# A seven-product feed-forward stage: another order of its twelve periods, and six weight chunks converted later

## The chip, the cores and the metric

The kernel runs on one core of one Trainium2 chip. The core's engines are TensorE (PE, with its weight loads as PEld), VectorE (DVE), ScalarE (ACT), GpSimd (POOL) and SyncE (SP); the last one issues nearly all transfers, on one queue. The metric is the device time of one execution in microseconds (us); lower is better. Before the change three runs took 952.39, 954.0 and 958.7 us, a median of 954.0 us.

## The reference

Attention over 4 batches of 576 tokens (8 heads of 64), then a gated block with a spatial matrix, then the block that the change is about. Cut to its end:

```python
def _moe2_ref(x, U, V, w_ch1, w_ch2):
    xt = x.transpose(0, 2, 1)
    h = xt @ U @ V
    u = x + h.transpose(0, 2, 1)
    ch = np.maximum(u @ w_ch1, 0.0) @ w_ch2
    return (u + ch).astype(np.float32)
```

Here x is 2304 tokens by 512 features, w_ch1 is 512 by 2048 and w_ch2 2048 by 512. The weights reach the device as 64-bit floats in raw words, and the kernel itself turns them into float32. Every product is made of three matmuls on a high and a low part of each operand.

## The kernel before, in words

The program has three stages. The **attention stage** (0 to 326 us) is written by hand and is not touched. In the **middle stage** (326 to 576 us) the gated block runs batch by batch: `u_step`, `v_step`, `s_step`, `o_step`, then `y_step`, `z_step`, `h_step` for x @ U @ V. TensorE's order is the order of the code there; the other engines' orders come from a scheduler. Beside it, `first_weights` converts the weights: 32 chunks of 128 rows by 512 numbers (`raw`), each with one ScalarE instruction (line 771) and four VectorE instructions (lines 772 to 775); after every second chunk four adds and subtracts (lines 782 to 785) complete seven combinations of blocks in the tile `cb`, two of them on VectorE and two on GpSimd, and `cb` is stored in DRAM (`combo`). `go` paces this: a chunk for every `EVERY` units of its clock.

The **channel stage** (`channel`, 576 to 954 us) computes the two big matrices by a seven-product scheme: instead of eight products of half-size blocks it makes seven, from combinations of the operands. The tokens are cut into 3 passes of 768, the hidden features into 4 weight groups of 512. A `period` is one pass with one group: 7 products with w_ch1 (tiles `r<i>x`, `r<i>y`, `r<i>z` in PSUM), then 7 with w_ch2 (`a<i>X`, and again y and z). A product is 12 matmuls. Before, period i took pass i // 4 and group i % 4, so every period ends with a change of weights, and two (after periods 3 and 7) with a change of pass as well.

- Change of weights (`split`): the seven combinations of both matrices come from `combo` in DRAM through four staging buffers (`YH`, `YL`, two each); ScalarE copies the high part (`w1h`, `w2h`, `setA`), VectorE or GpSimd subtracts to get the low part (`w1l`, `w2l`). For group 0, which returns at each change of pass, the low parts are not computed again: they were stored once (`lows`) and are loaded.
- Change of pass: VectorE makes four combinations of the next tokens (`tu`), ScalarE copies seven high parts and VectorE subtracts seven low parts into `setA`, `XH`, `XL`.

All work of the channel stage is put into one list by `at(t, fn)`, t in units of one product (14 per period), sorted by t; equal t keeps the order of entry. Each engine then works in that order, so an instruction that waits holds all that stand behind it on its engine. For example:

```python
            for t, fn in (
                (1.0, lambda: keep_sum("p1", "x")), (2.0, lambda: add_sum(1, "y", "p1")), (2.5, lambda: relu(1)),
                (3.0, lambda: keep_sum("u2", "x")), (3.4, lambda: high(1, T[1])), (3.9, lambda: low(pool, 1, T[1])),
                (4.0, lambda: keep_sum("p5", "z")), (5.0, lambda: add_sum(3, "x", "p5")),
```

`keep_sum` is a ScalarE copy out of PSUM. The copy of p5 must be done before the sixth product of the period (slot 5, from 5.0 units on) may add to z; the copy of u2 before the fifth (slot 4) may add to x.

The channel stage's first weights come through the tile `tmp` (14 loads, one per combination) as soon as the middle stage's tiles are free; behind their low parts on VectorE stand the four `X<-q` adds of the last but one batch, for which TensorE's transposes `t` wait.

Of the kernel before, what the change touches and what calls it, by code (L numbers as in the profile page):

```python
# [8 lines left out]
F32 = mybir.dt.float32  # L9
# [56 lines left out]
def tile_kernel(ctx: ExitStack, tc: tile.TileContext, qk, vv, tabs, w_in, g_ln, wsgT, b_sg, w_out, u_r, v_r, w1, w2, out):  # L66
# [8 lines left out]
    def bits(ap):  # L75

        return ap.bitcast(U32)
# [672 lines left out]
    LOWS = [dram.tile([P, 7, FG], F32, name=f"lows{c}", bufs=1) for c in range(2)]  # L750
    COMBO = [[dram.tile([P, 7, 2, HF], F32, name=f"combo{c}_{g}", bufs=1) for g in range(NG)] for c in range(2)]

    def first_weights():

        places = [{n: j for j, n in enumerate(at)} for at in (AT1, AT2)]
        jobs = []
        for g in range(NG):
            for c, src in enumerate((w1[:, g * 2 * FG:(g + 1) * 2 * FG], w2[g * FG:(g + 1) * FG])):
                for r in range(2):
                    jobs += [(g, c, r, k, src[k * P:(k + 1) * P]) for k in (r, r + 2)]  # L760
# [6 lines left out]
        def convert(j, t):  # L767

            raw = raws.pop(j).rearrange("p (a b) w -> p a b w", a=2)
            lo, hi, tu = raw[:, :, :, 0], raw[:, :, :, 1], bits(t)  # L770
            nc.scalar.activation(t, hi.bitcast(F32), AF.Abs)  # L771
            nc.vector.tensor_scalar(t, t, F64_LEAST, F64_MOST, ALU.max, ALU.min)
            nc.vector.tensor_scalar(tu, tu, 5, 2, ALU.logical_shift_left, ALU.logical_shift_right)
            nc.vector.scalar_tensor_tensor(tu, hi, 0xC0000000, tu, ALU.bitwise_and, ALU.bitwise_or)
            return nc.vector.scalar_tensor_tensor(tu, lo, 29, tu, ALU.logical_shift_right, ALU.bitwise_or)

        def combine(c, cb):
            at = places[c]
            e, o = nc.vector, nc.gpsimd
            op = {n: cb[:, at[n]] for n in range(1, 8)}  # L780
            a21, s1, s2, s4 = op[7], *((op[5], op[6], op[3]) if c == 0 else (op[5], op[6], op[3]))
            x = e.tensor_tensor(s1, a21, op[4], ALU.add)
            o.tensor_tensor(a21, a21, op[1], ALU.subtract)
            x = e.tensor_tensor(s2, s1, op[1], ALU.subtract)
            o.tensor_tensor(s4, op[2], s2, ALU.subtract)
            return x

        load(0)
        yield
        box = {}  # L790
        for j, (g, c, r, k, _) in enumerate(jobs):
            if j + 1 < len(jobs):
                load(j + 1)
            with ExitStack() as es:
                for x in LAST_D:
                    if x is not None:
                        es.enter_context(tc.issue_after(x.ins))
                at = places[c]
# [3 lines left out]
                m, n = ((1, 7), (2, 4))[k >= 2]  # L802
                LAST_D[0] = convert(j, cb[:, at[m]:at[n] + 1:at[n] - at[m]])
# [23 lines left out]
    def first_u():  # L827

        b11, b12, b21, b22 = (blk(i, j, 0) for i in range(2) for j in range(2))
        T = {}  # L830

        def combo(n, a, b):
            t = raw_tile()[:, :, :TB]
            sub(nc.vector, t, a, b)
            return t
        both = ((1, lambda: b11), (2, lambda: b21), (5, lambda: combo(5, b12, b11)), (6, lambda: combo(6, b22, T[5])),
                (4, lambda: combo(4, b21, T[6])), (7, lambda: combo(7, b12, b22)), (3, lambda: b22))
        for n, fn in both:
            x = T[n] = fn()
            copy(UOP[n][0], x)  # L840
            u_low(nc.gpsimd if n in (1, 2, 3) else nc.vector, n, x)

    def channel(before):

# [10 lines left out]
        def wop(c, n, x, r, a):  # L855
            j = (AT1, AT2)[c].index(n)
            o = r * HF + a * P
            return wslot(c, x, j)[:, o:o + P]

        def tmp():  # L860
            return p3.tile([P, 2, TB], F32, tag="tmp", name="tmp", bufs=6)

        def wide(t):
            return t[:, :, :TB]
# [17 lines left out]
        def split(c, g, j0, j1, t, stage, load, lo, e=None):  # L882
# [16 lines left out]
            at(t, high)  # L899
            if e is None:  # L900
                for a, b in parts:
                    at(lo, lambda a=a, b=b: nc.sync.dma_start(f(wslot(c, 1, a, b - a)), flat(LOWS[c][:, a:b])))
                return
            if e is nc.gpsimd:
                parts_low = [(j, j + 1) for j in range(j0, j1)]
# [3 lines left out]
                at(lo, lambda a=a, b=b: low(a, b))  # L909

        def stage_small():
            return p3.tile([P, 2, TB], F32, tag="tmp", name="tmp", bufs=6).rearrange("p a b -> p (a b)")

        turn = [0]

# [4 lines left out]

        def period(i):

            p, g = divmod(i, NG)
            o = 14 * i
            ps, T = {}, {}
            dve, act, pool = nc.vector, nc.scalar, nc.gpsimd
# [11 lines left out]
                copy(T[n], wide(ps[x]))  # L938

            def add_sum(n, x, m):  # L940
                T[n] = tmp()
                dve.tensor_tensor(T[n], wide(ps[x]), T[m], ALU.add)

            def relu(n):
# [24 lines left out]
            for t, fn in (  # L969
# [16 lines left out]
            if g == NG - 1:  # L986
                for t, a, b in ((12.5, 0, 1), (12.95, 1, 1), (13.4, 0, 0), (14.01, 1, 0)):
                    at(o + t, lambda a=a, b=b: leave(a, b))
            if i + 1 < NPASS * NG:
                h = (g + 1) % NG  # L990
                loads = (2.3, 4.0, 4.5, 6.5, 6.6) if i == 0 else (1.4, 1.8, 3.2, 3.5, 5.0)
                highs = (3.85, 5.45, 6.5, 9.0, 9.4) if i == 0 else (3.85, 4.75, 6.0, 7.0, 9.4)
                for c, j0, j1, load, t, lo, e in (
                    (0, 0, 2, loads[0], highs[0], 4.35, dve), (0, 2, 4, loads[1], highs[1], 10.3, pool),
                    (0, 4, 6, loads[2], highs[2], 11.6, pool), (0, 6, 7, loads[3], highs[3], 12.9, pool),
                    (1, 0, 2, loads[4], highs[4], 14.5, dve), (1, 2, 4, 11.65, 13.0, 15.08, dve),
                    (1, 4, 6, 13.0, 14.4, 16.5, dve), (1, 6, 7, 13.6, 15.4, 17.1, dve),
                ):
                    if h == 0:
                        split(c, h, j0, j1, o + t, stage, o + load, o + 7 * c + j1 + 0.05)  # L1000
                    else:
                        split(c, h, j0, j1, o + t, stage, o + load, o + lo, e)
            if g == NG - 1 and p + 1 < NPASS:
                b11, b12, b21, b22 = (blk(x, y, p + 1) for x in range(2) for y in range(2))
                U = {}

                def combo(n, a, b):
                    U[n] = pr.tile([P, 2, TB], F32, tag="tu", name="tu", bufs=2)
                    sub(dve, U[n], a() if callable(a) else a, b() if callable(b) else b)
                uh = lambda n, x: copy(UOP[n][0], x)  # L1010
                for t, fn in (
                    (1.7, lambda: uh(1, b11)), (2.1, lambda: uh(2, b21)), (2.5, lambda: u_low(dve, 1, b11)),
                    (2.95, lambda: u_low(dve, 2, b21)), (3.4, lambda: combo(5, b12, b11)), (3.85, lambda: combo(6, b22, U[5])),
                    (4.45, lambda: uh(6, U[6])), (5.25, lambda: uh(5, U[5])), (9.9, lambda: uh(3, b22)),
                    (14.5, lambda: u_low(dve, 6, U[6])), (14.95, lambda: u_low(dve, 5, U[5])),
                    (15.4, lambda: sub(dve, U[5], b12, b22)), (15.85, lambda: sub(dve, U[6], b21, U[6])),
                    (15.9, lambda: uh(7, U[5])), (16.45, lambda: u_low(dve, 7, U[5])), (16.8, lambda: uh(4, U[6])),
                    (16.9, lambda: u_low(dve, 3, b22)), (17.35, lambda: u_low(dve, 4, U[6])),
                ):
                    at(o + t, fn)  # L1020
            return ps

        for c in range(2):
            for j in range(7):
                t = -20 + 2 * (7 * c + j) / 2
                split(c, 0, j, j + 1, t, stage_small, t - 4, t + 0.5, nc.vector if j % 2 else nc.gpsimd)
                at(t + 4, lambda c=c, j=j: nc.sync.dma_start(LOWS[c][:, j], f(wslot(c, 1, j))))
        for i in range(NPASS * NG):
            ps = period(i)
            if i == 0:  # L1030
                before(at, ps)
# [175 lines left out]
```

## Time and profile before

| what | value |
|---|---|
| runs | 952.39, 954.0, 958.7 us |
| profiled execution | 956.1 us, of it 954.3 us span |
| TensorE busy | 895.8 us, 94% of the span |
| VectorE busy | 773.2 us, 81% |
| ScalarE, GpSimd busy | 492.6 us, 468.1 us |
| mean granted TensorE clock | 0.977 of full speed |

The page gives busy time per engine, and the chain that ended last: from 834 us on it is TensorE's products alone, one after the other. A timeline row reads: start, duration, engine, line, operation, written tile <- read tiles, shape, count, and in brackets the idle time of that engine just before and what ended it. SPq is SyncE's queue; its rows are issues of transfers, not their landing.

### The profile page before, as it was taken

To read this page: it belongs to the slowest core of one execution; us is meant where nothing else is said; L and a number is where in the kernel's file an instruction comes from. 1 tells how busy PE (TensorE), PEld (TensorE's weight loads), DVE (VectorE), ACT (ScalarE), POOL (GpSimd) and SP (SyncE) were. 2 spreads that over 40 slices of the span, in tenths; PEclk is the share of its full clock that TensorE was granted. 3 is DMA by queue.
4 is the path that set the end of the run, shared out by engine and by line. 5 is a ranking of instruction groups with operands and counts; after the bars stand their busy time and mean duration, and the time that the engine had idled before them with its cause. 6 is when DMAs were issued, how large, how long until landed. Compare 5 with 4: busy or idle time off the path is not lost. (4 is left out here: it accounts for less than half of the span.)

```text
span 954.3 us, 14383 instructions
## 1 busy us (share of the span) xinstructions
PE 895.8 (94%) x5279; PEld 811.3 (85%) x5279; DVE 773.2 (81%) x964; ACT 492.6 (52%) x749; POOL 468.1 (49%) x365
## 2 busy tenths in 40 slices
PE   9999999999999897997988759999999999799998
PEld 4677888788777897995988759999889999799997
DVE  6667799888995498997889965898879888887877
ACT  4565666676675634434324344445644565356441
POOL 6996777877644644553446441443114324032440
PEclk9999999999999998997999979999999999999999
DMA  6787876878633304654455284333772346634511
GB/s 194 195 198 179 212 205 158 215 169 188 177 102 110 111 8 151 195 167 144 153 170 175 83 295 150 111 101 113 229 265 79 117 137 218 213 118 136 155 56 67
DMA packets 90386, 148.33 MB, mean 155 GB/s; under 512 B 31606, under 2 KB 49292, under 8 KB 90316
## 3 DMA queue, kind: packets, MB, share of 16 engines
q1 hardware_dynamic: 90016, 147.34, 52.5%
q8 instruction: 42, 0.69, 0.3%
q14 instruction: 28, 0.23, 0.1%
q10 hardware_dynamic: 300, 0.08, 0.0%
HBM read 106.40 MB, written 23.14 MB: 136 GB/s over the span
## 5 line engine op out<-in xcount | busy, mean ns | idle before, releaser
L213 DVE TENSOR_REDUCE MX<-sm 128x1 f32<-128x576 f32 (+1 forms) x160 | 117.0, 747 | 37.4 <-PE sm L208 32.1
L277 PE MATMUL pv<-pc,VV 128*65 128x288 f32 (+1 forms) x516 | 145.7, 405 | 0.0
L250 PE MATMUL st<-Q,K 65*128 65x288 f32 (+3 forms) x640 | 126.5, 320 | 3.2 <-DMA Q<-mt 1.9
L250 PEld LDWEIGHTS st<-Q,K 65*128 65x128 f32 (+3 forms) x640 | 95.0, 178 | 18.0 <-DMA Q<-mt 2.5
L253 ACT ACTIVATE pc<-st 128x576 f32<-128x576 f32 x129 | 83.1, 645 | 31.5 <-PE st L250 29.1
L277 PEld LDWEIGHTS pv<-pc,VV 128*65 128x65 f32 (+1 forms) x516 | 69.2, 136 | 29.1 <-issue 0.2
L822 POOL TENSOR_TENSOR r7l<-tmp,r7h 128x768 fp32r<-128x768 f32 x12 | 25.6, 2130 | 126.5 <-ACT r7h L819 37.4
L822 POOL TENSOR_TENSOR r1l<-tmp,r1h 128x768 fp32r<-128x768 f32 x12 | 23.2, 1930 | 130.1 <-ACT r1h L819 110.0
L208 PE MATMUL sm<-K,Q 128*128 128x288 f32 (+1 forms) x320 | 72.1, 315 | 1.2 <-ACT pc L253 0.6
L172 POOL TENSOR_TENSOR Q<-raw,Q 128x576 fp32r<-128x576 f32 x30 | 45.7, 1523 | 30.1 <-ACT Q L167 30.0
L771 ACT ACTIVATE cb<-raw 128x512 f32<-128x512 f32 x32 | 21.5, 674 | 71.3 <-DMA raw<-in_w 61.4
L208 PEld LDWEIGHTS sm<-K,Q 128*128 128x128 f32 (+1 forms) x320 | 50.1, 178 | 7.3 <-DVE MX L213 0.9
L153 POOL TENSOR_TENSOR raw<-raw,tab 128x576 f32<-128x576 f32 x31 | 50.6, 1631 | 2.5 <-DMA raw<-in_qk 2.5
L330 DVE TENSOR_TENSOR X<-stage,rb 64x576 f32<-64x576 f32 x30 | 47.5, 1584 | 1.6 <-DMA rb<-rr 1.1
L155 POOL TENSOR_TENSOR raw<-raw 128x576 f32<-128x576 f32 x31 | 47.6, 1537 | 0.5
L587 PE MATMUL u<-XH,setA 128*128 128x288 f32 x256 | 47.6, 303 | 0.0
L154 POOL TENSOR_TENSOR raw<-raw,tab 128x576 f32<-128x576 f32 x31 | 44.4, 1431 | 0.0
L819 ACT ACTIVATE w2h<-YL 128x1024 fp32r<-128x1024 f32 (+1 forms) x22 | 18.6, 844 | 48.1 <-DMA YL<-combo 44.6
L587 PE MATMUL m<-WS,VH 128*128 128x288 f32 x192 | 34.6, 304 | 6.6 <-ACT ug L658 2.8
L587 PE MATMUL v<-setA,XH 128*128 128x512 f32 x128 | 39.6, 391 | 1.3 <-DVE X L689 1.3
L587 PEld LDWEIGHTS u<-XH,setA 128*128 128x128 f32 x256 | 39.8, 196 | 0.3
L819 ACT ACTIVATE w2h<-YH 128x1024 fp32r<-128x1024 f32 x22 | 23.2, 1056 | 31.3 <-DMA YH<-combo 20.1
(1111 smaller groups left out, 2630.2 us busy)
## 6 DMA issues: line engine op xcount, KB each, us to landing
YH<-combo SPq DMA_DIRECT2D x44, 512.0 KB
raw<-in_qk SPq DMA_DIRECT2D x31, 576.0 KB
raw<-in_w SPq DMA_DIRECT2D x32, 512.0 KB
combo<-cb SPq DMA_DIRECT2D x16, 896.0 KB
YL<-combo SPq DMA_DIRECT2D x22, 512.0 KB
K<-Q SPq DMA_DIRECT2D x30, 288.0 KB
YL<-combo SPq DMA_DIRECT2D x22, 256.0 KB
VV<-in_vv SPq DMA_DIRECT2D x16, 320.0 KB
```

Of the source, the lines that this page charges most:

```text
L153: lambda: e.tensor_tensor(raw[:, 0], raw[:, 0], tab[:, 0], ALU.mult),
L154: lambda: e.tensor_tensor(raw[:, 1], raw[:, 1], tab[:, 1], ALU.mult),
L155: lambda: e.tensor_tensor(raw[:, 0], raw[:, 0], raw[:, 1], ALU.add),
L172: nc.gpsimd.tensor_tensor(Q2[:, :S], rot, f(Q1), ALU.subtract)
L208: nc.tensor.matmul(ps[:TS[t], n, :HALF], Q1[:, t * P:t * P + TS[t]], K1[:, n * HALF:(n + 1) * HALF], start=True, stop=True)
L213: nc.vector.tensor_reduce(MXs[h % 2][:TS[t], t:t + 1], ps[:TS[t], :, :HALF], AX.XY, ALU.max)
L250: nc.tensor.matmul(ps[:kk, n, :HALF], l[:, c * P:c * P + kk], r[:, ns], start=st, stop=not st)
L253: nc.scalar.activation(h2(pc[:kk]), ps[:kk, :, :HALF], AF.Exp, scale=0.125)
L277: nc.tensor.matmul(o, l, r, start=(c == 0 and j == 0), stop=(c == NC - 1 and j == len(pr) - 1))
L330: nc.vector.tensor_tensor(X[b][rows, pr], STAGE.pop(h - 1 + a)[:D], RB[i][:, a], ALU.mult)
L587: nc.tensor.matmul(o, l, rr, start=(first and j == 0), stop=(last and j == n - 1))
L822: return e.tensor_tensor(out, a, b, ALU.subtract)
```

## The change

1. **Order of periods.** A table gives pass and group of each period: (0,0), (0,1), (0,2), (1,2), (1,0), (1,1), (2,1), (2,0), (2,2), (2,3), (0,3), (1,3). Four ends of periods change the pass and keep the weights (after 2, 5, 9 and 10); seven change the weights and keep the pass.
2. **Kept operands.** Low parts of groups 0 to 2 are stored (nine of fourteen slots each), and loaded when the group returns; the other five are computed again, on GpSimd. The token combinations of passes 0 and 1 are stored (`u`) and fetched when the pass returns, in periods 9 and 10.
3. **Conversion.** `EVERY` is 6.5 instead of 5.0, and only 26 of the 32 chunks are converted in the middle stage. The last six are converted in the channel stage, as twelve half chunks (`words`) at the times of `LATE`, with one buffer for the words and one for the combinations. All four combining operations run on VectorE.
4. The temporaries `tmp` have 4 buffers instead of 6; T[1] has a buffer of its own.

```diff
-    EVERY = 5.0
+    EVERY, EARLY = 6.5, 26
...
+    ORDER = [(0, 0), (0, 1), (0, 2), (1, 2), (1, 0), (1, 1), (2, 1), (2, 0), (2, 2), (2, 3), (0, 3), (1, 3)]
+    KEPT = [(0, 0), (0, 1)] + [(1, j) for j in range(7)]
...
+    def combine(c, cb):
+        at = PLACES[c]
+        e = nc.vector
+        op = {n: cb[:, at[n]] for n in range(1, 8)}
+        a21, s1, s2, s4 = op[7], op[5], op[6], op[3]
+        e.tensor_tensor(s1, a21, op[4], ALU.add)
+        e.tensor_tensor(a21, a21, op[1], ALU.subtract)
+        e.tensor_tensor(s2, s1, op[1], ALU.subtract)
+        return e.tensor_tensor(s4, op[2], s2, ALU.subtract)
...
+    LATE = (1, 0.1), (3, 0.1), (4, 0.1), (4, 2.1), (4, 4.1), (5, 0.1), (6, 2.0), (6, 3.9), (7, 0.1), (7, 2.1), (7, 4.1), (8, 0.1)
...
-            p, g = divmod(i, NG)
+            p, g = ORDER[i]
+            q, h = ORDER[i + 1] if i + 1 < len(ORDER) else (p, g)
...
+            if i > 0 and g not in [x for _, x in ORDER[:i]] and g < NG - 1:
+                for c, j in KEPT:
+                    at(o + (0.05 if c == 0 else 3.5), lambda c=c, j=j: nc.sync.dma_start(LOWS[c][g][:, j], f(wslot(c, 1, j))))
+            if h != g:
+                fresh = h not in [x for _, x in ORDER[:i]]
...
-                    if h == 0:
+                    if fresh or (c, j0) not in KEPT:
+                        split(c, h, j0, j1, o + t, stage, o + load, o + lo, e)
+                    else:
                         split(c, h, j0, j1, o + t, stage, o + load, o + 7 * c + j1 + 0.05)
...
+                def fetch(n):
+                    U[n] = block()
+                    nc.sync.dma_start(U[n], UKEPT[q][n])
...
+        def fetch(m):
+            raws[m] = pr.tile([P, HF, 2], U32, tag="words", name="words", bufs=1)
+            nc.sync.dma_start(raws[m].rearrange("p n w -> p (n w)"), parts[m][3])
...
+        def done(m):
+            c, r, _, _ = parts[m]
+            combine(c, cbs[m // 4])
+            nc.sync.dma_start(COMBO[c][NG - 1][:, :, r], cbs[m // 4])
+        at(10.0, lambda: fetch(0))
+        for m, t in enumerate(LATE):
+            t = 14 * t[0] + t[1]
+            at(t - 0.1, lambda m=m: begin(m))
+            at(t, lambda m=m: raws[m][1]())
+            if m + 1 < len(parts):
+                at(t + 1.0, lambda m=m: fetch(m + 1))
+            if m % 4 == 3:
+                at(t + 0.75, lambda m=m: done(m))
```

`begin` is the ScalarE instruction of a half chunk, `raws[m][1]` its four VectorE instructions.

How the orders change, at three places. First ScalarE in the middle stage, second batch, about 434 to 444 us of the trace: `ug<-v` are the activations of `v_step`, `cb<-raw` the conversions, `YH<-t` the copies for which the next `z_step` waits. Before:

```order
L771 ACTIVATE cb<-raw 128x512
L578 ACTIVATE ug<-v_2_4557 128x1024
L578 ACTIVATE ug<-v_4_4620 128x512
L771 ACTIVATE cb<-raw 128x2x256
L710 ACTIVATE YH<-t_0_4656 128x1024
L710 ACTIVATE YH<-t_2_4669 128x1024
L771 ACTIVATE cb<-raw 128x2x256
```

Now:

```order
L578 ACTIVATE ug<-v_2_4543 128x1024
L773 ACTIVATE cb<-raw 128x512
L578 ACTIVATE ug<-v_4_4606 128x512
L710 ACTIVATE YH<-t_0_4634 128x1024
L710 ACTIVATE YH<-t_2_4647 128x1024
L639 ACTIVATE ug<-ug,bmv,brs 128x512 x2
```

The conversion that stood right ahead of `YH<-t` stands one activation earlier, and the next one behind.

Second VectorE at the end of the middle stage, about 556 to 574 us of the trace. `X<-w` are the adds after `o_step`, `w1l`, `setA`, `w2l` low parts of the channel stage's first weights, `X<-q` the adds that the transposes wait for. Before:

```order
L689 TENSOR_TENSOR X<-w_1_5633,X 128x576
L822 TENSOR_TENSOR w1l<-tmp,w1h 128x512
L689 TENSOR_TENSOR X<-w_2_5670,X 128x576
L822 TENSOR_TENSOR w1l<-tmp,w1h 128x512
L822 TENSOR_TENSOR setA_71<-tmp,setA_70 128x512
L689 TENSOR_TENSOR X<-w_3_5696,X 128x576
L822 TENSOR_TENSOR w2l<-tmp,w2h 128x512 x3
L738 TENSOR_TENSOR X<-q_0_5817,X 128x576
```

Now:

```order
L689 TENSOR_TENSOR X<-w_2_5635,X 128x576
L829 TENSOR_TENSOR XH<-raw,XH 128x768
L689 TENSOR_TENSOR X<-w_3_5661,X 128x576
L829 TENSOR_TENSOR w1l<-tmp,w1h 128x512 x2
L829 TENSOR_TENSOR setA_71<-tmp,setA_70 128x512
L829 TENSOR_TENSOR w2l<-tmp,w2h 128x512 x3
L738 TENSOR_TENSOR X<-q_0_5777,X 128x576
```

All six low parts now stand behind the last `X<-w`.

Third the start of period 4 as it is now. ScalarE (`tmp<-r4x` the copies of p1 and u2, `tmp<-r4z` that of p5):

```order
L826 ACTIVATE w2h<-YL 128x512
L773 ACTIVATE cb_6111<-words 128x256
L826 ACTIVATE t_6933<-t_6933 128x768
L826 ACTIVATE tmp<-r4x 128x768
L826 ACTIVATE r1h<-t_6933 128x768
L826 ACTIVATE w1h<-YH 128x1024
L773 ACTIVATE cb_6981<-words 128x256
L826 ACTIVATE tmp<-r4z 128x768
```

and SyncE's queue at the same place:

```order
L1071 DMA words<-in_w 128x512
L901 DMA YH<-combo_1_3345 128x1024
L901 DMA YL<-combo_1_3345 128x1024
L914 DMA w1l<-lows_1_3325 128x1024
L1083 DMA combo_3_3347<-cb_6111 896x1x256
L1071 DMA words<-in_w 128x512
```

Two half chunks stand among ScalarE's copies, the second one directly ahead of p5; its fetch stands behind the store of the combination that ends with the half chunk before it.

## Rows read from the trace of the kernel before

**Rows 1.** The page: span, and busy time of each engine with its instructions.

```profile
span 954.3 us, 14383 instructions
PE 895.8 (94%) x5279; PEld 811.3 (85%) x5279; DVE 773.2 (81%) x964; ACT 492.6 (52%) x749; POOL 468.1 (49%) x365
```

**Rows 2.** Windows, middle stage: length, busy by engine, granted clock, DMA share, GB/s.

```profile
326.16:575.62 249.46, 216.69 (x1404) 203.97 (x1404) 213.57 (x302) 99.67 (x152) 120.52 (x103) 0.93 0.46 152
440.00:460.00 20.00, 16.32 (x94) 14.84 (x95) 12.77 (x22) 10.23 (x16) 6.32 (x8) 0.75 0.36 126
```

**Rows 3.** Timeline, 430 to 444 us: fetches of raw chunks and what waited.

```profile
430.63 0.33 SPq L765 DMA_DIRECT2D raw<-in_w  x1
...
433.97 0.69 ACT L771 ACTIVATE cb<-raw 128x512 f32<-128x512 f32 x1 [4.84 <-DMA raw<-in_w]
434.32 0.53 SPq L806 DMA_DIRECT2D combo<-cb  x1
...
434.96 2.54 SPq L765 DMA_DIRECT2D raw<-in_w  x2
...
441.59 0.66 ACT L771 ACTIVATE cb<-raw 128x512 f32<-128x512 f32 x1 [5.53 <-DMA raw<-in_w]
...
443.21 0.80 PE L726 MATMUL z<-YH,U 128*128 128x512 f32 x1 [6.39 <-ACT YH L710]
```

**Rows 4.** Groups of the conversion (busy, mean ns), and lines by min/median/max ns.

```profile
L772 DVE TENSOR_SCALAR cb<-cb 128x512 f32<-128x512 f32 x32 | 22.4, 699 | 6.5 <-ACT cb L771 6.4
L775 DVE SCALAR_TENSOR_TENSOR cb<-raw,cb 128x512 uint32<-128x512 uint32 x32 | 28.4, 889 | 0.7
L783 POOL TENSOR_TENSOR cb<-cb 128x256 f32<-128x256 f32 x16 | 15.2, 951 | 39.5 <-DVE cb L782 23.6 <-issue 15.5 <-POOL XL L431 0.4
L775 DVE SCALAR_TENSOR_TENSOR cb<-raw,cb x32: 674/692/2221, 355.2 to 541.0; 128x512 uint32<-128x512 uint32 x32
L782 DVE TENSOR_TENSOR cb<-cb x16: 393/423/1533, 359.3 to 543.3; 128x256 f32<-128x256 f32 x16
```

**Rows 5.** Timeline, 562 to 575 us: the start of the channel stage.

```profile
563.18 0.74 DVE L689 TENSOR_TENSOR X<-w,X 128x576 f32<-128x576 f32 x1
...
567.04 0.44 SPq L889 DMA_DIRECT2D tmp<-combo  x1
...
571.49 2.75 DVE L738 TENSOR_TENSOR X<-q,X 128x576 f32<-128x576 f32 x4
571.51 0.63 ACT L819 ACTIVATE w2h<-tmp 128x512 fp32r<-128x512 f32 x1 [0.67 <-DMA tmp<-combo]
...
572.29 3.03 PE L708 MATMUL t<-ident,X 128*128 128x128 f32 x13 [7.78 <-DVE X L738]
```

**Rows 6.** Timeline of PE, both changes of pass: first matmuls of halves of periods.

```profile
670.40 0.51 PE L877 MATMUL r3x<-setA,w1h 128*128 128x384 f32 x2
...
709.25 0.98 PE L877 MATMUL r4x<-setA,w1h 128*128 128x384 f32 x2 [2.13 <-ACT tmp L819]
...
721.37 0.52 PE L877 MATMUL a4X<-r1h,w2h 128*128 128x384 f32 x2
...
736.05 0.51 PE L877 MATMUL r5x<-setA,w1h 128*128 128x384 f32 x2
...
794.73 0.51 PE L877 MATMUL r7x<-setA,w1h 128*128 128x384 f32 x2
...
846.47 0.52 PE L877 MATMUL a8X<-r1h,w2h 128*128 128x384 f32 x2
```

**Rows 7.** Timeline, 701 to 708 us: a staged block and the copy that waited.

```profile
701.90 0.44 SPq L889 DMA_DIRECT2D YH<-combo  x1
...
707.45 1.06 ACT L819 ACTIVATE w2h<-YH 128x1024 fp32r<-128x1024 f32 x1 [5.60 <-DMA YH<-combo]
```

**Rows 8.** Groups of the channel stage: one VectorE add, one ScalarE copy.

```profile
L963 DVE TENSOR_TENSOR X<-a3X,X 128x768 f32<-128x768 f32 x4 | 3.8, 956 | 1.2 <-PE a3X L877 1.1
L819 ACT ACTIVATE r3h<-tmp 128x768 fp32r<-128x768 f32 x12 | 10.2, 846 | 15.9 <-DVE tmp L942 15.9
```

More of the change, by code (lines that the diff above doesn't have):

```diff
@@ L765, in load @@
             return nc.sync.dma_start(raws[j].rearrange("p n w -> p (n w)"), jobs[j][-1])
[L767 to L786, printed above, removed]
         load(0)
@@ L790, in first_weights @@
         box = {}
-        for j, (g, c, r, k, _) in enumerate(jobs):
-            if j + 1 < len(jobs):
+        for j, (g, c, r, k, _) in enumerate(jobs[:EARLY]):
+            if j + 1 < EARLY:
                 load(j + 1)
@@ L797, in first_weights @@
                         es.enter_context(tc.issue_after(x.ins))
-                at = places[c]
+                at = PLACES[c]
                 if k < 2:
@@ L801, in first_weights @@
                 cb = box[0]
-                m, n = ((1, 7), (2, 4))[k >= 2]
-                LAST_D[0] = convert(j, cb[:, at[m]:at[n] + 1:at[n] - at[m]])
+                m, n = BLOCKS[k >= 2]
+                begin, rest = words(raws.pop(j).rearrange("p (a b) w -> p a b w", a=2), cb[:, at[m]:at[n] + 1:at[n] - at[m]])
+                begin()
+                LAST_D[0] = rest()
                 if k >= 2:
@@ L858, in wop @@
             return wslot(c, x, j)[:, o:o + P]
+        TMPS = 4
         def tmp():
-            return p3.tile([P, 2, TB], F32, tag="tmp", name="tmp", bufs=6)
+            return p3.tile([P, 2, TB], F32, tag="tmp", name="tmp", bufs=TMPS)
         def wide(t):
@@ L911, in stage_small @@
         def stage_small():
[L912 removed]
+            return tmp().rearrange("p a b -> p (a b)")
         turn = [0]
@@ new lines, in period @@
+            if q == p:
+                return ps
+            U = {}
+            uh = lambda n, x: copy(UOP[n][0], x() if callable(x) else x)
+            block = lambda: stage()[:, :2 * TB].rearrange("p (a b) -> p a b", a=2)
+            if q in [x for x, _ in ORDER[:i]]:
+                def fetch(n):
+                    U[n] = block()
+                    nc.sync.dma_start(U[n], UKEPT[q][n])
+                for n, load, t, lo in (
+                    (1, 0.6, 1.9, 3.5), (2, 1.15, 2.4, 3.95), (6, 2.55, 3.95, 4.4), (5, 3.15, 4.6, 14.1), (7, 4.1, 5.4, 14.55),
+                    (3, 4.5, 6.3, 15.0), (4, 4.95, 7.2, 15.45),
+                ):
+                    at(o + load, lambda n=n: fetch(n))
+                    at(o + t, lambda n=n: uh(n, U[n]))
+                    at(o + lo, lambda n=n: u_low(dve, n, U[n]))
+                return ps
@@ new lines, in period, with combo @@
+            b11, b12, b21, b22 = (blk(x, y, q) for x in range(2) for y in range(2))
+            def combo(n, a, b):
+                U[n] = block()
+                sub(dve, U[n], a() if callable(a) else a, b() if callable(b) else b)
+                if q < len(UKEPT):
+                    nc.sync.dma_start(UKEPT[q][n], U[n])
+            x = {1: b11, 2: b21, 3: b22, 5: lambda: U[5], 6: lambda: U[6], 7: lambda: U[7], 4: lambda: U[4]}
+            get = lambda n: x[n]() if callable(x[n]) else x[n]
@@ L1021, in period @@
+            parts = {5: (b12, b11), 6: (b22, lambda: U[5]), 7: (b12, b22), 4: (b21, lambda: U[6])}
+            for k, t in times.items():
+                n = int(k[1])
+                at(o + t, {"T": lambda n=n: combo(n, *parts[n]), "h": lambda n=n: uh(n, x[n]), "l": lambda n=n: u_low(dve, n, get(n))}[k[0]])
+            if q < len(UKEPT):
+                for n in (1, 2, 3):
+                    at(o + 13.0, lambda n=n: nc.sync.dma_start(UKEPT[q][n], x[n]))
             return ps
```

69 lines of the change are left out of this document (37 added, 32 removed).

## The prediction

> **What bounds the kernel now.** I read the page's busy times first, then the windows by stage, then the timeline where TensorE stops. TensorE is busy 94% of the span [rows 1], so a gain can only come from places where it waits or runs at the lower of its two clock levels (1.2 and 2.4 GHz). There are three.
>
> In the middle stage TensorE is busy 216.7 of 249.5 us, VectorE 213.6 [rows 2]: 32.8 us of idle, and both engines near 86%, so neither alone sets the pace. Two stops are large. At 443 us TensorE waits 6.39 us for ScalarE's copy `YH`, and ScalarE itself stood 5.53 us in front of a conversion whose raw words had not come [rows 3]. After it the window from 440 us shows a mean granted clock of 0.75 [rows 2]. At 572 us it waits 7.78 us for VectorE's `X<-q` [rows 5].
>
> At the changes of pass, from the first product of period 3 to the second half of period 4, 670.40 to 721.37, 50.97 us pass for three halves; a half without a change takes 736.05 − 721.37 = 14.68 us [rows 6], which is seven products of 2.10 us. Three are 44.0, so this change costs 6.9 us. The other one, 794.73 to 846.47, costs 51.74 − 44.0 = 7.7. Inside, TensorE waits 2.13 us for ScalarE's copy of p1 [rows 6], and that copy stood behind `w2h<-YH`, whose block landed only 5.55 us after its issue, ScalarE idle all that time [rows 7].
>
> **The change part by part.** The sum is made against the profiled execution, 956.1 us (span 954.3 and 1.8 around it), which is 2.1 us above the median of the runs.
>
> *Changes of pass.* The two changes that came together with a change of weights go: **−14.6 us**. The four new ones have no staged weights beside them, so ScalarE's copies of p1 and p5 stand behind no landing in periods 3 and 6, and the same four `tu` and seven low parts on VectorE fit in what the weights' low parts leave free there: nothing. If that cover fails, the price is what it was: 12 us at worst remain saved. In periods 9 and 10 the token parts are fetched, seven blocks each; the first two high parts now stand between p1 and u2 on ScalarE and are due 2 to 3 us after their buffers come free, while a landing takes 3.3 us or more [rows 3]: **+1.5** in all (0 to 4). The stores of kept parts lie on SyncE's queue beside products that wait for none of them: nothing.
>
> *Middle stage.* Six chunks leave. The lines 772 and 775 take 699 and 889 ns on average [rows 4], the two between are within 0.08 us of these, so a chunk is 3.2 us of VectorE, six 19.2. Three combinations leave with them (2 × 0.42 each, 2.5 us), and for the other 13 two operations come over from GpSimd: 26 × 0.42 = +10.9, by the median of line 782 [rows 4]. Then contention: line 775 has a median of 692 and a mean of 889 ns [rows 4], so about 0.2 us too much on each of 128 conversion instructions, 25 us; GpSimd's 32 combining operations (0.95 us each [rows 4], 30 us) are a quarter of its 120.5 us [rows 2], so a quarter of the excess goes: −6. In sum VectorE is relieved of 17 us. As both engines are at 86%, I let half of it reach the path: −8. The stop at 443 us is apart from this: of the two conversions that stood ahead of `YH` there, one moves behind it, and fetches come less often behind a store; of the 6.39 us and the 4.1 us that the clock costs ((1 − 0.75) × 16.3 us busy [rows 2]) I take 7. Together **−15** (bounds −6 and −22).
>
> The Trainium skill (SBUF — State Buffer, "Who interferes with whom") says that VectorE with two SBUF inputs and GpSimd exclude each other for whole instructions rather than share. By that rule the relief would be larger than by the excess in the rows; it is the second rival below.
>
> *Start of the channel stage.* Before, `X<-q` began 8.3 us after the last `X<-w` (563.18 to 571.49 [rows 5]), as two of the low parts had been made earlier. Now all six stand behind the last `X<-w`, and there are four buffers: load 6 needs the buffer of load 2, which the first of these low parts frees, so loads 6 to 13 run in two rounds of four. A round is a landing (3.3 us for a raw chunk of twice the size on a free queue [rows 3], 4.5 us for the last `tmp` load on a full one, 567.04 to 571.51 [rows 5]; fewer stores stand beside it, so I take 3.8), a copy of 0.63, a low part of about 1 and an issue of 0.4: 5.9. Two rounds and the first low part are 12.5: **+4** (0 to 7).
>
> *Half chunks among ScalarE's copies.* This is the part that decides. A half chunk is 128x256; its four VectorE instructions cost between half of the clean 128x512 ones (1.1 us) and four at 0.42 (1.7): 1.5. Its words are half a raw chunk: the nearest rows are 3.3 and 4.5 us, I take 3.5. Behind the 896 KB store a raw chunk took 6.6 us (434.96 to 441.59 against 430.63 to 433.97 [rows 3]); half a chunk, 5. Period 4, from its first product on: last add of the period before 0.95 [rows 8], third half chunk until 2.5, fetch issued 2.9, landed 6.4, fourth half chunk's copy 6.8, its VectorE part 8.3, four combining operations 10.0, store issued 10.5, next fetch 10.9, landed 16, copy 16.4, and only then p5, 0.85 [rows 8]: 17.2. TensorE wants to write z in slot 5, at 5 × 2.10 = 10.5. That is a wait of 6.7. Period 7 is the same without the store: fetch at 8.7, landed 12.2, p5 at 13.4: 2.9. In period 8 a store stands ahead of the first staged block (4.6 + 6.6, a copy of 1.1, p5: 13.2): 2.7. In period 6 the fetch goes out earlier: 1. Sum **+13** (bounds 3, all landings short, and 24, all at 6.6 us).
>
> The Trainium skill (DMA: Bandwidth & Descriptors, "Anatomy of one DMA") gives 2.0 us and bytes over 436 GB/s, so an estimate of 2.6 us for the words; by it these four places would cost about 5 us less and the sum would be some 938. No row here shows a landing that short.
>
> Sum: 956.1 − 14.6 + 1.5 − 15 + 4 + 13 = 945.0; less 2.1 for the median, **943 us**, 1.2% faster.
>
> **The rivals.**
> - *The half chunks hide* (933 us): fetches land before ScalarE gets there, the 13 become 3. For it: ScalarE is busy only 52% [rows 1]. Against: the order puts the second half chunk directly ahead of p5, and its fetch behind a store that ends no sooner than 10 us into the period.
> - *VectorE is freed by more* (935 us): each GpSimd combining operation held VectorE's two-input instructions for all of its 0.95 us [rows 4]. Then up to 30 us come off VectorE instead of 6; a third of the other 24 on the path makes the middle stage's 15 into 23. For it: conversions of up to 2.2 us where the median is 0.69 [rows 4]. Against: TensorE's own work bounds what is left, 32.8 us of idle [rows 2], of which 7.78 [rows 5] stay. The Trainium skill's page SBUF — State Buffer, cited above, would have it so.
> - *The middle stage hardly gains* (953 us): in its last stretch, from the third batch's `o_step` on, there are still seven chunks and now 16 combining operations on VectorE instead of 8. If that stretch is VectorE's, what was saved ahead of it is given back: −5 instead of −15.
> - *Slower* (970 us): the wait in period 4, and its like in 6, 7 and 8, is long enough that the clock falls each time. Place: p5 behind `cb<-words`. With all landings at 6.6 us the four waits are 24, and if each is followed by what the 6.39 us stop was (4.1 us, [rows 2, 3]), 16 more: 40 instead of 13. Waits and clock together must pass 34 us to make it over 1% slower, 24 to be slower at all. Against: periods 6 and 8 wait for little.
>
> **How the numbers follow.** Chances: my forecast 0.32, half chunks hidden 0.22, VectorE freed by more 0.12, middle stage without gain 0.20, slower 0.14. A measurement of this kernel tells about 1%, 9.5 us, from no change. Faster by over 1% (under 944.5) are the two better rivals and 0.20 of my forecast's 0.32: 0.54. Slower by over 1% is the last rival: 0.14. The rest, 0.32, is within 1%. The range leaves out the slower rival and the far ends of the better ones: 923 to 961 us.
>
> **What would show it.** Right: no half of a period above 15.5 us where the pass changes (after periods 2 and 5); a stop of TensorE at slot 5 of period 4 for ScalarE's copy of `r4z`, with `cb<-words` waiting for its words ahead of it, 5 to 8 us; smaller ones in 7 and 8; TensorE's transposes `t` before the channel stage waiting about 12 us rather than 7.78 for `X<-q`; the middle stage some 11 us shorter up to there. Wrong: periods 4, 7 and 8 at 29.4 us; a middle stage as long as before, with VectorE still busy at 86%; or periods 9 and 10 that wait for fetched token parts by more than 2 us each.

## The result: 964.7 us, 1.1% slower

| | before | after |
|---|---|---|
| median of 10 runs each | 955.2 us | 964.7 us |
| ratio, 95% interval | | 1.0109 [1.0077, 1.0142] |
| profiled execution | 956.1 us | 970.9 us |
| first product of the channel stage | 575.62 us | 570.46 us |
| from there to the first product of `a11` | 359.1 us | 379.0 us |

943 us was forecast, so the sign was wrong. The middle stage and the start of the channel stage together gained 5.2 us, and the channel stage behind them lost 19.9. The profiled execution is 6.2 us above its own median; times below compare places within profiles. Of the 14.8 us between the two profiles 2.0 lie in the attention stage, which the change does not touch: the first matmul of the middle stage comes at 328.17 us, and came at 326.16 before (324.2 to 326.8 in the other traces read below).

The page of after, the lines that answer to [rows 1]:

```profile
span 969.0 us, 14314 instructions
PE 902.4 (93%) x5279; PEld 816.1 (84%) x5279; DVE 759.6 (78%) x1004; ACT 477.2 (49%) x733; POOL 424.0 (44%) x323
```

Windows of after, columns as in [rows 2]: the middle stage, then period 4's first half up to the end of its stop, the 6 us behind the stop, an undisturbed half, and the 6 us behind the stop of period 6:

```profile
326.16:570.46 244.30, 213.68 (x1404) 202.42 (x1404) 199.45 (x302) 98.32 (x150) 90.61 (x71) 0.93 0.42 137
699.63:719.04 19.41, 11.03 (x61) 10.39 (x60) 8.70 (x17) 8.38 (x13) 1.88 (x1) 0.84 0.74 251
719.04:725.17 6.13, 6.13 (x24) 6.13 (x25) 4.49 (x6) 2.90 (x4) 0.00 (x0) 0.67 0.33 131
725.17:740.01 14.84, 14.84 (x85) 14.84 (x85) 13.65 (x15) 5.61 (x8) 9.44 (x6) 1.00 0.48 149
783.77:789.63 5.86, 5.86 (x25) 5.86 (x25) 4.85 (x8) 2.78 (x4) 0.00 (x0) 0.71 0.51 145
```

VectorE's busy time in the middle stage fell by 14.1 us (213.57 in [rows 2]), and the stage by 5.2. Behind the stop TensorE is busy all the time, at a mean granted clock of 0.67 between its two levels: 6.13 × 0.33 is 2.0 us, on top of the stop.

Timeline of after, period 4: two fetches of half chunks, the sums' store between them, and the row of instructions on ScalarE that stood behind the second. This is what [rows 3] and [rows 7] showed elsewhere:

```profile
703.33 0.33 SPq L1071 DMA_DIRECT2D words<-in_w  x1
...
706.41 0.43 ACT L773 ACTIVATE cb<-words 128x256 f32<-128x256 f32 x1 [2.31 <-DMA words<-in_w]
...
711.80 0.53 SPq L1083 DMA_DIRECT2D combo<-cb  x1
712.43 0.59 SPq L1071 DMA_DIRECT2D words<-in_w  x1
717.86 0.43 ACT L773 ACTIVATE cb<-words 128x256 f32<-128x256 f32 x1 [7.91 <-DMA words<-in_w]
718.20 0.79 ACT L826 ACTIVATE tmp<-r4z 128x768 f32<-128x768 f32 x1
...
719.04 2.93 PE L889 MATMUL r4z<-XH,setA 128*128 128x384 f32 x8 [8.33 <-ACT tmp L826]
```

Read it backwards: TensorE waits 8.33 us for the copy that empties z (p5); that copy is ready to run, but ScalarE works in order and stands in front of `cb<-words`, whose words were fetched behind an 896 KB store and were there 5.4 us after their issue (712.43 to 717.86). TensorE stops at the same place in periods 6, 7 and 8; each stop is shown with the transfer and the ScalarE instruction that stood ahead of the copy:

```profile
775.87 0.33 SPq L1071 DMA_DIRECT2D words<-in_w  x1
781.65 0.43 ACT L773 ACTIVATE cb<-words 128x256 f32<-128x256 f32 x1 [2.67 <-DMA words<-in_w]
783.77 2.33 PE L889 MATMUL r6z<-XH,setA 128*128 128x384 f32 x8 [2.54 <-ACT tmp L826]
...
812.13 0.33 SPq L1071 DMA_DIRECT2D words<-in_w  x1
816.69 0.43 ACT L773 ACTIVATE cb<-words 128x256 f32<-128x256 f32 x1 [3.09 <-DMA words<-in_w]
817.88 2.34 PE L889 MATMUL r7z<-XH,setA 128*128 128x384 f32 x8 [2.65 <-ACT tmp L826]
...
843.69 0.53 SPq L1083 DMA_DIRECT2D combo<-cb  x1
844.27 0.65 SPq L901 DMA_DIRECT2D YH<-combo  x1
850.57 1.06 ACT L826 ACTIVATE w1h<-YH 128x1024 fp32r<-128x1024 f32 x1 [3.13 <-DMA YH<-combo]
852.38 2.61 PE L889 MATMUL r8z<-XH,setA 128*128 128x384 f32 x8 [2.39 <-ACT tmp L826]
```

In periods 6 and 7 it is again a half chunk whose words have not landed. In period 8 it is a staged block, issued behind the sums' store and copied 6.3 us after its issue. Each of these three halves is 4.0 to 4.4 us longer than an undisturbed one: the stop, and 1.7 us of lower clock behind it (5.86 × 0.29; the rows behind the other two read 0.71 as well).

Timeline of after, start of the channel stage, to be held against [rows 5]:

```profile
547.70 7.98 SPq L901 DMA_DIRECT2D tmp<-combo  x8
548.45 0.75 DVE L689 TENSOR_TENSOR X<-w,X 128x576 f32<-128x576 f32 x1
...
566.32 2.74 DVE L738 TENSOR_TENSOR X<-q,X 128x576 f32<-128x576 f32 x4
...
567.13 3.67 PE L708 MATMUL t<-ident,X 128*128 128x128 f32 x16 [17.35 <-DVE X L738]
```

The last `X<-w` came 14.7 us earlier than before (563.18; 16.7 earlier if each is counted from the first matmul of its middle stage), `X<-q` only 5.2: 17.9 us lie between them now, where 8.3 lay before.

### The profile page after: what moved, and what is told of

The parts are those of the page before. It is cut to its first block, busy times and chain, and to the rows that moved or that the text cites. A ratio compares the mean times of both kernels' runs of the same rounds, so it can differ in the third digit from the quotient of the medians.

```text
span 969.0 us, 14314 instructions
## 1 busy us (share of the span) xinstructions
PE 902.4 (93%) x5279; PEld 816.1 (84%) x5279; DVE 759.6 (78%) x1004; ACT 477.2 (49%) x733; POOL 424.0 (44%) x323
## 5 line engine op out<-in xcount | busy, mean ns | idle before, releaser
L829 POOL TENSOR_TENSOR r1l<-t,r1h 128x768 fp32r<-128x768 f32 x12 | 22.4, 1864 | 150.5 <-ACT r1h L826 150.5
L773 ACT ACTIVATE cb<-raw 128x512 f32<-128x512 f32 x26 | 17.4, 674 | 53.0 <-DMA raw<-in_w 52.1
L540 POOL TENSOR_TENSOR GL<-g,GH 128x576 fp32r<-128x576 f32 x16 | 25.1, 1569 | 37.4 <-ACT GH L672 37.4
L293 ACT ACTIVATE stage<-pv 65x576 f32<-65x576 f32 x31 | 20.0, 647 | 30.2 <-PE pv L277 30.2
```

The lines of the kernel that those rows point to most:

```text
L829: return e.tensor_tensor(out, a, b, ALU.subtract)
```

## The experiments

Medians in us, ratios to the kernel before with 95% intervals.

| run | median | ratio |
|---|---|---|
| a1_words2 | 954.2 | 0.9995 [0.9977, 1.0014] |
| a2_early32 | 944.8 | 0.9890 [0.9869, 0.9911] |
| a3_ustore_act | 962.2 | 1.0078 [1.0058, 1.0098] |
| a5_late_gap | 977.3 | 1.0235 [1.0213, 1.0257] |
| b1_combine_dve | 951.2 | 0.9961 [0.9941, 0.9981] |
| b2_eight_lone | 949.8 | 0.9941 [0.9914, 0.9968] |
| b3_adds_first | 938.1 | 0.9828 [0.9803, 0.9853] |
| b4_five_tiles | 943.2 | 0.9882 [0.9856, 0.9907] |
| c1_store_later | 940.8 | 0.9856 [0.9801, 0.9910] |
| c2_eight_first | 932.9 | 0.9763 [0.9717, 0.9809] |
| c3_first_five | 937.1 | 0.9808 [0.9764, 0.9852] |
| c4_third_moved | 959.9 | 1.0054 [1.0030, 1.0077] |

**No half chunks at all (a2_early32).**

```diff
-    EVERY, EARLY = 6.5, 26
+    EVERY, EARLY = 5.0, 32
-    LATE = (1, 0.1), (3, 0.1), (4, 0.1), (4, 2.1), (4, 4.1), ...
+    LATE = ()
```

> The changed kernel with no half chunks at all: all 32 chunks are converted in the middle stage again, one in 5.0 of its steps as before the change; the new order of periods, the kept operands, 4 staging tiles and the combinations on VectorE stay. Theory A: the channel stage from its first product on is about 394 - 26 = 368 us (374 before less the 14.6 of pass changes, plus fetches); the middle stage takes back what the six fewer chunks gave (15 us); the wait for the first transpose of the channel stage stays about 17 us: about 953. Theory C (order of periods or kept operands cost): channel stage stays at 380 or more, 965 or more.

Measured 944.8. From the first product on, 350.5 us against 379.0: the twelve half chunks cost 28.5 us of the profile, and the channel stage starts only 3.3 us later without them (573.71). Theory C falls. Theory A had 953, because it let the middle stage take back 15 us and not 3.3. The 28.5 are those of a profile 6.2 us above its median; that of a3_ustore_act, below, has the same half chunks, is 1.0 us above its own median and shows 375.0 us for the same stretch, so 24.5. The changes of pass can be read clean here, first matmuls as in [rows 6]:

```profile
669.57 0.52 PE L889 MATMUL r3x<-setA,w1h 128*128 128x384 f32 x2
...
714.04 0.52 PE L889 MATMUL a4X<-r1h,w2h 128*128 128x384 f32 x2
...
788.27 0.51 PE L889 MATMUL r7x<-setA,w1h 128*128 128x384 f32 x2
...
832.63 0.52 PE L889 MATMUL a8X<-r1h,w2h 128*128 128x384 f32 x2
```

44.47 and 44.36 us instead of 50.97 and 51.74: −13.9.

**Two landing places for the words (a1_words2).** The second is the slots of the sums' tile that are written last.

```diff
+            if m % 2:
+                raws[m] = bits(sums(m)[:, 2:4]...)
...
-                at(t + 1.0, lambda m=m: fetch(m + 1))
+                at(t + 1.0 + m % 4 // 3, lambda m=m: fetch(m + 2))
```

> The changed kernel with one edit: the half chunks' words have two landing places in turn (the tile of their own, and the two slots of the sums' tile that are written last), so that each is fetched about 3 slots (6 us) before its Abs on ScalarE rather than 1. Places of the conversions, staging and order of periods as in the change. Theory A (the channel stage loses its gain because ScalarE stands before a half chunk that has not landed, with its copies of sums p5 and u2 behind): TensorE's stops before r4z (8.33 us), r6z (2.54), r7z (2.65), r8z (2.39) go, with the lower clock behind them; the first half of period 4 goes from 25.5 to about 17-19 us, those of 6, 7 and 8 each by 2 to 4 us; in all 13 to 18 us less, about 949 against 964.7. Theory B (the half chunks cost by the time of their own instructions on ScalarE and VectorE, landed or not): under 4 us less, about 962. Theory C (the new order of periods or the kept operands slow the stage): no change.

10.5 us less, not the 13 to 18 of Theory A; period 4's first half fell to 22.07 and period 7's stop went, but period 8's stayed (2.15 us), as no half chunk makes it. The rest of period 4's stop is another wait:

```profile
706.95 0.53 SPq L1089 DMA_DIRECT2D combo<-cb  x1
...
712.50 0.43 ACT L773 ACTIVATE cb<-words 128x256 f32<-128x256 f32 x1 [5.12 <-DMA combo<-cb]
...
713.68 2.93 PE L889 MATMUL r4z<-XH,setA 128*128 128x384 f32 x8 [4.65 <-ACT tmp L826]
```

The words are there, but the ScalarE instruction of the half chunk (`cb<-words`, the "Abs" of the expectations) writes into the one tile of sums, which the store still reads. So the place had two locks, and the landing was only the later one.

**Only the third half chunk of period 4 moved (c4_third_moved).**

```diff
-    LATE = ... (4, 4.1), (5, 0.1), ...
+    LATE = ... (4, 13.4), (5, 6.6), ...
```

> The changed kernel with two of the twelve half chunks moved: the third of period 4 from 4.1 to 13.4 of the period (its Abs then stands behind the copies of p5 and u2), and the one after it from 0.1 to 6.6 of period 5. By the prediction's own term (a stop of 6.7 us in period 4): 6 to 7 us less, about 958. By the stop that the changed kernel's trace shows (8.3 us, 10.9 with the lower clock behind it): 10 to 11 less, about 954. If another wait takes its place (the staging load behind the sums' store, as with the lone half chunks): r4z still stops for 3 to 5 us, 959 to 961.

Period 4's first half fell from 25.54 to 14.76, so the stop and all that hung on it went, 10.8 us; the two moved half chunks then cost 2.1, 0.6 and 1.4 us in the three halves behind it, so 6.8 are left. The medians differ by 4.8 only. The time, 959.9, lies in the range of the third case, but not by its mechanism: `r4z` does not stop at all.

**All half chunks behind p5 (a5_late_gap), a miss.**

```diff
+    LATE = (1, 4.15), (1, 11.6), (2, 4.15), (2, 11.6), ... (6, 4.15), (6, 11.6)
```

> The changed kernel with other places for the half chunks alone: two in each of periods 1 to 6, at 4.15 (behind ScalarE's copy of sum p5) and at 11.6 of a period's 14 slots, 6.5 to 7.5 slots apart, so that each has landed and none stands ahead of the copies of p5 and u2. Theory A: the stops of 8.3, 2.5, 2.6 and 2.4 us and the lower clock behind them go: 20 to 26 us less, about 941 against 964.7. Theory B (their own instructions cost, wherever they stand): half chunks add about 1 us each to their halves again, under 10 us less, about 956. Theory C: no change.

12.6 us more instead of 20 to 26 less. The stops of z went with one exception (r3z, 2.39 us). New ones of 3.6 us came at the end of periods 1, 3, 4 and 6, and one of 3.8 at r5x. Why r5x stops is open. At the four ends VectorE's four operations at 11.6 of the period stand ahead of the sum `X<-a1X`, for which the last product waits. Rows of VectorE, GpSimd and TensorE in period 1:

```profile
631.88 1.38 DVE L769 TENSOR_SCALAR cb<-cb 128x256 f32<-128x256 f32 x1
633.30 1.27 DVE L770 TENSOR_SCALAR cb<-cb 128x256 uint32<-128x256 uint32 x1
634.60 1.39 DVE L771 SCALAR_TENSOR_TENSOR cb<-words,cb 128x256 uint32<-128x256 uint32 x1
636.02 0.42 DVE L772 SCALAR_TENSOR_TENSOR cb<-words,cb 128x256 uint32<-128x256 uint32 x1
636.37 0.95 DVE L976 TENSOR_TENSOR X<-a1X,X 128x768 f32<-128x768 f32 x1
```

```profile
631.11 2.01 POOL L829 TENSOR_TENSOR w1l<-YH,w1h 128x512 fp32r<-128x512 f32 x1
633.07 1.34 POOL L829 TENSOR_TENSOR setA<-YH,setA 128x512 fp32r<-128x512 f32 x1
634.37 1.34 POOL L829 TENSOR_TENSOR setA<-YL,setA 128x512 fp32r<-128x512 f32 x1
```

```profile
637.46 0.59 PE L889 MATMUL a1X<-r4h,w2h 128*128 128x384 f32 x2 [3.58 <-DVE X L976]
```

I had looked at ScalarE alone when I chose these places.

**Eight lone half chunks (b2_eight_lone), then the sums' store later (c1_store_later).**

```diff
-    EVERY, EARLY = 6.5, 26
+    EVERY, EARLY = 5.8, 28
+    LATE = (1, 0.1), (2, 0.1), (3, 0.1), ... (8, 0.1)
```

> The changed kernel with 28 chunks converted in the middle stage, one in 5.8 of its steps, and eight half chunks in the channel stage, one in each of periods 1 to 8 at 0.1 of it, each fetched some 13 slots (27 us) ahead and none behind a store of the sums' tile. Theory A (what made half chunks dear was that they came 2 slots apart, behind a landing and behind the store that still read the one sums' tile): each costs 0.3 to 1 us of its half, 3 to 8 us in all over the run without any; the channel stage starts 2 to 5 us earlier; about 947, against 944.8 with no half chunk and 964.7 with twelve. Theory B (a half chunk costs 2 us wherever it stands): 956 to 960. If they are free: 941.

Measured 949.8, between the theories. Against a2_early32 the first halves of periods 1, 2, 6 and 7 cost 0 to 0.2 us, of 3 and 5 1.7 and 0.5, but of 4 and 8, where the sums are stored, 7.9 and 6.1. Period 4:

```profile
697.24 0.53 SPq L1083 DMA_DIRECT2D combo<-cb  x1
...
698.51 1.06 SPq L901 DMA_DIRECT2D YH<-combo  x1
...
705.83 1.06 ACT L826 ACTIVATE w1h<-YH 128x1024 fp32r<-128x1024 f32 x1 [5.44 <-DMA YH<-combo]
706.79 0.79 ACT L826 ACTIVATE tmp<-r4z 128x768 f32<-128x768 f32 x1
...
707.64 2.93 PE L889 MATMUL r4z<-XH,setA 128*128 128x384 f32 x8 [5.23 <-ACT tmp L826]
```

No half chunk stands before p5 here. A staged block does, issued behind the store and copied 7.3 us after its issue. The next edit moves that store alone:

```diff
+                at(t + 3.55, lambda m=m: leave_sums(m))
```

> The run with eight lone half chunks (949.75 us) with one edit: the store of the sums' tile (896 KB, after the fourth half chunk of a pair) is issued 2.8 slots later, in periods 4 and 8 at 3.65 of the period instead of 0.85, behind the staging loads of the first weights and no longer ahead of them in SyncE's queue. Theory D (in periods 4 and 8 the staging loads land behind that store, ScalarE stands before its copy w1h<-YH for 5.4 us and its copy of sum p5 stands behind it): the first halves of periods 4 and 8 go from 22.7 and 20.9 us to 15-16.5, 10 to 13 us less in all, about 938. Theory A alone (it is the Abs, the four operations of a half chunk and the combination on VectorE, before the sum t<-r4y): no change, 949.

940.8 us, 9.0 less where 10 to 13 were expected; the first halves of periods 4 and 8 are whole again, 14.75 and 14.76 us, and `w1h<-YH` waits for nothing:

```profile
692.50 0.51 PE L889 MATMUL r4x<-setA,w1h 128*128 128x384 f32 x2
...
707.25 0.52 PE L889 MATMUL a4X<-r1h,w2h 128*128 128x384 f32 x2
```

Theory D holds. Eight half chunks now cost 2.6 us in all (353.1 against 350.5 us from the first product to that of `a11`).

**The start.** First the stores that I took for the cause (a3_ustore_act):

```diff
-            nc.sync.dma_start(UKEPT[0][n], x)
+            nc.scalar.dma_start(UKEPT[0][n], x)
```

> The changed kernel with one edit: the seven stores of the first pass's token parts are issued on ScalarE, right behind its own copy of the same tile, and no longer on SyncE ahead of the first weights' loads. Theory S (SyncE stood before those stores, waiting for VectorE's differences, so that the staging loads began 15 us later against the last conversion than before): the loads begin some 10 us earlier, TensorE's wait before its transposes goes from 17.35 to 8-11 us, about 957 against 964.7. Rival (four staging tiles instead of six, or the low parts left to VectorE and GpSimd, set the start): the wait shrinks by less than 3 us, about 963.

Theory S falls: TensorE's wait is 17.31 us as before the edit. The first staging load still goes out 1.0 us ahead of the last `X<-w` (543.87 and 544.87), and SyncE's wait there is now 3.8 us for the last store of the sums. From the first load to `X<-q` it is 18.9 us, against 18.6 in the changed kernel and 20.1 in a2_early32.

Five staging tiles (b4_five_tiles):

```diff
-        TMPS = 4
+        TMPS = 5
```

> The run with all chunks converted early (944.8 us) with five staging tiles instead of four. If the staging loads of the first weights wait for a tile that GpSimd's low parts free (SyncE's waits for w1l, w2l and setA there sum to 8 us), the start comes 1 to 3 us earlier: 942 to 944. If the loads follow one another at the rate of the transfers, or VectorE and GpSimd at their own: no change, 944.5 to 945.5.

943.2; the first product comes 3.5 us earlier (570.25), and 2.7 us are lost again in period 10 of this profile, at a wait of r10x for ScalarE. Then what stands behind the low parts (b3_adds_first):

```diff
-        at(-3.0, lambda: run(h_step, a, *range(KT)))
-        at(-1.0, lambda: run(y_step, b, 0, 2))
+        at(-13.2, lambda: run(h_step, a, *range(KT)))
+        at(-12.9, lambda: run(y_step, b, 0, 2))
```

> The run with all chunks converted early (944.8 us), and one edit at the start of the channel stage: VectorE's four sums that empty the q tiles, and the two transposed tiles behind them, are put ahead of the split of the second weights (between the first weights' parts and w2's) instead of behind all of it. Theory Q (TensorE's wait of 11.3 us before its transposes is for PSUM that those sums empty, and the sums stand behind low parts that wait for staging loads): the transposes begin near 561 us instead of 570.4, the first product near 565 instead of 573.7, of which 2 to 4 us are given back where the first copies stand behind w2's; 937 to 941. Rival (the loads of the first weights set the start, so the first product waits for its weights all the same): under 2 us, 943 or more.

938.1, 6.8 less. Theory Q holds: the transposes wait 2.53 us, not 11.31, the first product comes at 563.80, and 3.2 us of it are given back at r0x, whose copy stands behind w2's:

```profile
559.67 2.74 DVE L738 TENSOR_TENSOR X<-q,X 128x576 f32<-128x576 f32 x4
...
560.47 3.67 PE L708 MATMUL t<-ident,X 128*128 128x128 f32 x16 [2.53 <-DVE X L738]
...
573.16 0.62 PE L889 MATMUL r0x<-setA,w1h 128*128 128x384 f32 x2 [1.92 <-ACT tmp L826]
```

**What the rest of the change is worth (b1_combine_dve).** The kernel before, with this alone:

```diff
-            e, o = nc.vector, nc.gpsimd
+            e, o = nc.vector, nc.vector
```

> The kernel before with one edit: the four combinations of a chunk pair all on VectorE, as the change has it, rather than two there and two on GpSimd. With it, the run with all chunks converted early (944.8 us) divides into this part and the new order of periods. Theory 1 (the combination on VectorE takes away a hand-over to GpSimd and its return, and little else): 952 to 956, so that the order of periods with its kept operands is worth about 10 of the 10.5 us. Theory 2 (VectorE is what the middle stage waits for, so two more instructions a pair cost): 958 to 962, and the order is worth 15.

951.2, 3.4 less (3.7 by the ratio), a little better than either theory. No trace of this run is read, so where the time goes is not shown. The order of periods with all that belongs to it is then worth 6.4 us (951.2 to 944.8; 6.8 by the ratios), not 10.

**Put together.** c3_first_five is b3_adds_first with `TMPS = 5`, c2_eight_first is c1_store_later with the two lines of b3_adds_first.

> All chunks early, VectorE's q sums first (938.05 us), with five staging tiles instead of four. If the loads of w2's parts, which come in a row behind the tiles' release, still set the first half's stop (1.9 us before r0x there) and the two gains add: 935 to 937. If the first product no longer waits for a staging tile: 938.

> The run with the later store (28 chunks early, eight lone half chunks) with the start of the run that has VectorE's q sums and the transposed tiles ahead of the split of the second weights. If both gains add (10 to 13 us by the store, 6 to 7 by the start): 930 to 934. If the start is set by the first weights' loads once the middle stage is shorter: 936 to 939. If the store still delays: 943.

937.1, 1.0 less than without the fifth tile, and 932.9, where both gains add. The second is 2.4% faster than the kernel before: the change's own idea, with eight late half chunks for twelve, and one store and two steps at other places.

## Why the prediction was wrong

**Changes of pass, −14.6: right.** −13.9. The token parts fetched in periods 9 and 10 cost 3.2 us, not 1.5 (847.47 to 909.41 in a2_early32 against 861.31 to 920.02), within the bounds.

**Middle stage, −15: right where I read it, and that was the wrong end.** The last `X<-w` came 14.7 us earlier, 16.7 from the stage's own start. Both parts of the term are there: VectorE's busy time fell by 14.1 us (17 forecast), and the stop of 6.39 us at 443 us is 0.29 us now, with 1.58 us for VectorE's `YL` behind it (440.06 and 442.15); what each of them gave, and so how far the −15 was luck, is not shown. But the channel stage hangs on another chain: last store of the sums, first staging load, split, `X<-q`. The store went out 4.6 us sooner, the load only 0.6. Before:

```profile
547.64 0.51 SPq L806 DMA_DIRECT2D combo<-cb  x1
548.26 11.49 SPq L889 DMA_DIRECT2D tmp<-combo  x8
```

After:

```profile
543.00 0.51 SPq L813 DMA_DIRECT2D combo<-cb  x1
546.24 0.51 SPq L848 DMA_DIRECT2D u<-raw  x1
547.70 7.98 SPq L901 DMA_DIRECT2D tmp<-combo  x8
```

A store of token parts stands between the two now, and where it does not (a3_ustore_act) SyncE waits 3.8 us for the sums' store to end; why the first load did not need that before is open. The load's time is that of a single execution: four runs whose middle stage is unchanged or nearly so (a1, a3, a5, c4) show it at 543.3 to 545.7, so 2.5 to 4.9 us earlier. The fewer chunks were also spread wider (26 × 6.5 = 169 on the clock that spaces them, 32 × 5.0 = 160); with 28 × 5.8 = 162, so with two chunks more, the load went out at 540.45 (b2_eight_lone).

**Start of the channel stage, +4 (bounds 0 to 7): failed,** +9.6. I counted two rounds of four loads behind the last `X<-w`, as if the others had gone out ahead of it, like before (15 us ahead). They went out 0.75 us ahead, so the whole chain of fourteen loads stood there, 18.6 us from the first load to `X<-q`. What the term had wrong is the path: b3_adds_first, which takes `X<-q` out from behind the second half of that chain, has the transposes wait 2.53 us instead of 11.31. The two readings belong together: −15 and +4 were meant to give −11, and the first product came 5.2 us earlier.

**Half chunks, +13 (bounds 3 and 24): the step that decided.** 28.5 us in this profile, 24.5 in that of a3_ustore_act. The path in period 4 was the forecast one; the size of the term was not. From the period's first product, forecast and then measured: first fetch 2.9, 3.7; store 10.5, 12.2 (one combining operation took 2.06 us); next fetch 10.9, 12.8; landed 16, 18.2; the stop 6.7, 8.3. The second lock, the store that still reads the tile of sums, I had not seen; it alone still stopped z for 4.65 us in a1_words2. The four stops were 13.3 in the sum and are 15.9. What the sum had at nothing is the lower clock behind them: 2.0, 1.7, 1.7 and 1.7 us, 7.1 in all. I had priced it at the 443 us stop, used it in the slower rival, and not in my own term. That price, 4.1 us, was too high as well, since its window begins 3.2 us before that stop ends; behind the stop, from 443.21 to 449.50, the granted clock was 0.50 and TensorE busy 5.82 us, so it cost 2.9 us.

The four halves that I put at 13 in sum cost 10.8, 4.3, 4.5 and 4.1 more than in a2_early32, and periods 2, 3, 5 and the second half of 7, which I put at nothing, another 4.4. A landing as short as the 2.6 us that stand behind the 938 us of the prediction did come, 2.55 us at 807.49, but the landings that made the stops took 5.4, 5.8, 4.6 and 6.3. The section of the Trainium skill cited there (DMA: Bandwidth & Descriptors, "Anatomy of one DMA") fits its figures to transfers that GpSimd issues; these are issued on SyncE.

**The rivals.** "Slower" (970 us, chance 0.14) named the place, p5 behind `cb<-words`, and the clock, and 964.7 lies nearest to it. But it had 40 us for waits and clock, and 28.5 are measured. By its own working that would not make the kernel 1% slower (34 us needed); it did because the stages ahead gave 5.2 us and not 11. "The middle stage hardly gains" falls as it was put, since the last `X<-w` came 14.7 us earlier and not 5. "VectorE is freed by more" falls: its busy time fell by less than my own 17 us. "Half chunks hide" was possible: c1_store_later is it, with eight half chunks and 2.6 us.

Summed over the profiles: −13.9 + 3.2 − 14.7 + 9.6 + 28.5 = 12.7, of the 14.8 between 956.1 and 970.9; the 2.0 us that the attention stage took longer lie in the −14.7. The other 2 us are undisturbed halves, mostly 14.76 to 14.84 us instead of 14.64 to 14.76; a2_early32 has them too, at a granted clock of 1.00. Why is open.

## What to carry to other kernels

Before work is put on an engine that works in order, list what stands behind it there, and for each input the latest of all it waits for: the landing, the buffer's last reader, and what is ahead in the transfer queue. A stage has gained only where the chain that opens the next one has moved, so read its length at the first instruction of that next stage. When the sum holds a stop of some us, it must also hold the lower clock behind it (here 1.7 to 2.0 us behind stops of 2.4 to 8.3 us), at the price of a stop of like length in the trace, read from the stop's end on.

## What the runs showed of the hardware

VectorE's small operations took 1.27 to 1.39 us instead of 0.28 to 0.43 (the run with half chunks behind p5, above), each ending 0.1 to 0.3 us after the GpSimd operation beside it. GpSimd's ends are rough, but the pattern holds three times in a row, and again for the 2.06 us in period 4 of the changed kernel (709.25 to 711.31, GpSimd's r1l to 711.02). The Trainium skill (SBUF — State Buffer, "Who interferes with whom") has VectorE's two-input operations, and its one-input ones in a two-port mode, wait out, as a whole, a GpSimd operation that reads SBUF and started first. The rows with two inputs agree; the two one-input operations do if they ran in such a mode, which no run here shows.

Words of 256 KB for which ScalarE stood waiting came 2.55, 3.08, 4.56 and 5.78 us after their issue in the changed kernel where no store was ahead of them, each with staging loads issued 0.4 us behind it, and 5.43 us behind an 896 KB store. Why four like places differ by 3 us is open. A 512 KB block issued 1.3 us behind such a store was copied 7.3 us after its issue, by a ScalarE that waited for nothing else; with the store issued later this wait was gone (c1_store_later).
